# Chunked attention feeding a snake MLP: key blocks at pitch 128, memory keys first, one load per block

## The chip, the cores and the metric

One Trainium2 chip, one core of it. The metric is the time of one execution in microseconds of device time, the median of the runs of a kernel. Its engines are TensorE (PE in the profile, its weight loads PEld), VectorE (DVE), ScalarE (ACT), GpSimd (POOL) and SyncE (SP), which run side by side and wait for each other through semaphores. SP, ACT and POOL also issue DMA transfers. Matrix results land in PSUM, which has 8 banks.

## The reference

```python
# q, k, v: (4, 8, 768, 64); mem_k, mem_v: (4, 8, 8, 64); f32
for c in range(S // 32):                       # chunks of 32 queries
    l_start, r_end = max(0, 32 * c - 16), min(S, 32 * c + 32 + 8)
    k_full = concat(mem_k, k[l_start:r_end])   # 8 memory rows, 16 left, 32 own, 8 right
    v_full = concat(mem_v, v[l_start:r_end])
    a = softmax(q_c @ k_full.T / 8)
    out[32 * c:32 * c + 32] = a @ v_full
x = out.transpose(0, 2, 1, 3).reshape(3072, 512)
h = x @ w_in                                   # w_in: (512, 2048)
g = h + sin(alpha * h) ** 2 / alpha
result = g @ w_out                             # w_out: (2048, 512)
```

## The kernel before

**Attention.** The 768 queries of a batch are taken in 8 blocks `j` of 96 (three chunks). A block needs 8 memory keys and 120 sequence keys, from 16 rows before it to 8 after it, together 128. Scores are computed with keys on partitions and queries on columns: the stationary operand is a slice of 128 columns of `kT` (keys transposed, 64 dims of two heads on 128 partitions), the moving one 96 columns of `qT`. What a chunk may not see is masked by a bias of the exponential (`biasm`, batches 1 to 3, `scores`) or by an extra matmul with `mrow` and `mind` (batch 0, `u_scores`). The value rows of the same 128 keys stand in `vw`, one column of ones beside 64 values, so that `values` (or `u_values`) gives numerators and sums in one matmul; `normed` (DVE, a reciprocal and a multiply) makes `x_blk`, which is transposed into `xT` by TensorE and a copy (words `t`, `T`) or by a DMA transpose from SP (word `c`).

**Layout.** For batches 0 and 1, `kT` holds the sequence with the 8 memory keys repeated every 104 columns, so that neighbouring blocks share columns and a block's slice starts at 104 j; memory keys stand in the middle, at rows 64 to 72 of a block. `vw` and `kst` have the same order: rows 0 to 64, memory, rows 72 to 128. Each is filled by two loads, 64 and 56 rows high.

**How k and q are turned.** Batches 0 and 1: rows lie as `(p r)` with r = 6 on 128 partitions (`k_bf`, `q_bf`); `turn` makes 12 TensorE transposes for a pair of heads `hp` into one PSUM bank, `put_k` (one copy, and a small one for the ends) and `put_q` put them into place. Batch 0's k and q come as f32 by SP (`load_f`, eight loads) and are cast by ACT and DVE (word `a`); batch 1's are cast in the DMA by POOL (`load_one`). Batches 2 and 3: `row_loads` brings rows by POOL into `kst` (16 loads of k) and `qst` (6 of q), `mem_rows` adds the memory keys, and `crosses` turns them by 14 DMA transposes from SP.

**The MLP.** For a batch and one of 16 tiles `ft` of 128 hidden units: `half_tile` (L424) makes 4 matmuls of 384 columns for each half of the batch, `sine` (ACT, L439) takes sin, `squared` squares it on ACT (L444), DVE or POOL (L447), `finish` (DVE, L451) writes `gT` and frees the tile's pair of banks. `second` (L462) makes 96 matmuls of 512 columns per batch, and `close` copies the sum out and stores it.

**The order** is written by hand, as words that `Stage.run` follows; each engine works through its own instructions in that order. Stage -1 is the start and batch 0's attention; stage i is batch i's MLP with batch i+1's attention in it; stage 3 has no attention, and the rest of `second` follows it. Words: `b4`, `h4` the halves of tile 4 (`h` also its sine), `q4A` its square and on which engine (A, V = DVE, P = POOL), `g4` its finish; `f7` seven matmuls of the batch's `second`; `k1 l1` turns of heads 2 and 3, `K1V L1A` their copies; `s24` scores and exponentials of blocks 2 and 4, `v4` values and normalization; `V024` V of batch 0, heads 2 to 4; `I02` w_in tiles 0 and 1; `U12` w_out; `dk108` batch 1's k; `dm` mem_v; `m0` memory values into `vw`; `R2` two of the `row_loads`, `Z` the memory rows, `X8` eight `crosses`; `z1` a dummy matmul on zeros; `Cb` and the like constants.

## Time and profile before

| | |
|---|---|
| time, median of 3 runs | 219.95 us (219.74 to 222.44) |
| span of the profiled execution | 218.5 us; its own time is not listed apart, the median lies 1.45 us above the span |
| TensorE busy | 203.2 us, 93% |
| ScalarE, VectorE, GpSimd busy | 143.6, 140.7, 99.0 us |
| DMA packets | 95908, of them 84864 under 512 bytes |
| POOL's DMA queue | 68736 packets, 13.25 MB |
| the other queue (SP, ACT) | 26976 packets, 14.62 MB |
| first MLP matmul (L424) | 25.14 us from the span's start |
| MLP stages 0, 1, 2, 3 start | 25.1, 75.9, 122.4, 173.3 us |

The page gives the busy time of each engine, then the span in 40 slices of 5.46 us with tenths of busy time (9 is 90% or more) and the granted TensorE clock, then DMA, the chain of waits that ended last, the costliest groups of instructions and the DMA issues. A group's line has its busy time, the mean of one in ns, and after the bar the idle time of the engine just before them and what ended it. Matmuls are pipelined, so the distance of starts, not the mean of one, is what a matmul costs.

### The profile page before, as it was taken

The numbers are of one execution on the slowest core, as the hardware profiler recorded it, in microseconds if no ns is written. First come the engines' busy times: TensorE is split into PE (matmuls) and PEld (weight loads), VectorE is DVE, ScalarE is ACT, GpSimd is POOL, SyncE is SP. The second block draws the span as 40 slices with busy tenths as digits, with TensorE's granted clock in tenths as the row PEclk, the third lists the DMA queues.
The fourth block names the chain that finished last, engine by engine and source line by source line (L and its number), as shares of the span: only waits on it lengthen the run. The fifth ranks groups of instructions, "written<-read, shape, count | busy, mean of one in ns | idle before, by whom it ended". The sixth has DMA issues, their size and how long they took to land.

```text
span 218.5 us, 4460 instructions
## 1 busy us (share of the span) xinstructions
PE 203.2 (93%) x1702; PEld 115.7 (53%) x1721; DVE 140.7 (64%) x218; ACT 143.6 (66%) x230; POOL 99.0 (45%) x140
## 2 busy tenths in 40 slices
PE   0999899999999999999999999994999999999994
PEld 0666655655455555554455555542455465654453
DVE  6697688999353669958577399991165277955010
ACT  2478988977838579969815598865457189892110
POOL 8949506498596490039960087598000004200000
PEclk9999999999999999999999999998899999999999
DMA  6999999999999799939995489999165410000312
GB/s 206 311 167 145 200 209 204 205 153 171 151 179 115 148 143 152 154 74 140 175 188 86 123 75 147 158 89 115 58 154 122 102 51 0 1 3 0 144 48 96
DMA packets 95908, 28.19 MB, mean 129 GB/s; under 512 B 84864, under 2 KB 92432, under 8 KB 95888
## 3 DMA queue, kind: packets, MB, share of 16 engines
q0 software_dynamic: 68736, 13.25, 87.2%
q1 hardware_dynamic: 26976, 14.62, 28.8%
q8 instruction: 13, 0.21, 0.4%
q10 hardware_dynamic: 176, 0.04, 0.1%
q14 instruction: 7, 0.06, 0.1%
HBM read 29.66 MB, written 6.29 MB: 165 GB/s over the span
## 4 chain that ended last, share of the span: by engine, by line
PE 64%; DMA 14%; DVE 7%; POOL 6%; issue 4%; ACT 3%; DVEq 0%; POOLq 0%
PE ps L462 36%; PE ps L424 22%; DMA vw<-in_v_dram 5%; DMA qT<-q_bf 3%; DVE gT L451 3%; DMA q_bf<-in_q_dram 3%; PE ps L414 3%; PE ps L385 2%; DMA kT<-kst 2%; DVE s L447 2%; POOL s L447 2%; ACT u L439 2%; PE ps L366 1%; DMA kst<-in_k_dram 1%; POOL vw L172 1%
## 5 line engine op out<-in xcount | busy, mean ns | idle before, releaser
L462 PE MATMUL ps<-w_out_sb,gT 128*128 128x512 bf16 (+1 forms) x382 | 88.6, 375 | 1.3 <-issue 0.3
L424 PE MATMUL ps<-xT,w_in_sb 128*128 128x384 bf16 x512 | 85.9, 326 | 0.7 <-DVE gT L451 0.5
L451 DVE SCALAR_TENSOR_TENSOR gT<-s,inv_alpha,ps 128x768 bf16<-128x768 f32 x64 | 63.0, 1012 | 12.5 <-ACT s L444 5.2
L424 PEld LDWEIGHTS <-w_in_sb 128*128 128x128 bf16 x512 | 49.7, 98 | 35.2 <-issue 1.8
L439 ACT ACTIVATE u<-ps,alpha_sb 128x768 f32<-128x768 f32 x64 | 56.6, 894 | 16.8 <-PE ps L424 14.3
L462 PEld LDWEIGHTS <-gT 128*128 128x128 bf16 x400 | 37.6, 99 | 38.4 <-issue 2.5
L447 POOL TENSOR_TENSOR s<-u 128x768 f32<-128x768 f32 x11 | 17.4, 1581 | 75.0 <-ACT u L439 75.0
L399 ACT ACTIVATE pt<-ps,biasm 128x256 bf16<-128x256 f32 x72 | 27.3, 488 | 12.1 <-PE ps L385 12.1
L469 DVE COPY o_sb<-ps 128x512 f32<-128x512 f32 (+1 forms) x15 | 9.9, 669 | 32.4 <-PE ps L462 30.5
L447 DVE TENSOR_TENSOR s<-u 128x768 f32<-128x768 f32 x23 | 21.9, 954 | 7.7 <-ACT u L439 7.6
L444 ACT ACTIVATE s<-u 128x768 f32<-128x768 f32 x30 | 25.0, 841 | 0.5
L354 DVE TENSOR_TENSOR x_blk<-ps,rinv 96x512 bf16<-96x512 f32 x32 | 22.0, 686 | 1.1
L469 ACT COPY o_sb<-ps 128x512 f32<-128x512 f32 (+1 forms) x10 | 5.7, 572 | 24.9 <-PE ps L462 24.9
L172 POOL DMA_DIRECT2D vw<-in_v_dram x13 | 12.6, 970 | 8.3 <-PE ps L366 5.3
L353 DVE RECIPROCAL rinv<-ps 96x8 f32<-96x8 f32 x32 | 6.4, 199 | 13.3 <-PE ps L414 12.7
L232 POOL DMA_DIRECT2D kst<-in_k_dram x16 | 11.7, 734 | 1.9 <-DMA vw<-in_v_dram 1.3
L179 POOL DMA_DIRECT2D vw<-in_v_dram x13 | 12.5, 958 | 0.0
L238 POOL DMA_DIRECT2D kst<-in_k_dram x16 | 11.7, 730 | 1.6 <-DMA vw<-in_v_dram 1.4
L369 ACT COPY xT<-ps 128x384 bf16<-128x384 bf16 x12 | 5.6, 495 | 8.0 <-PE ps L366 8.0
L245 POOL DMA_DIRECT2D q_bf<-in_q_dram x12 | 10.7, 909 | 0.0
L414 PEld LDWEIGHTS <-pt 128*128 128x128 bf16 x192 | 8.2, 97 | 4.2 <-ACT pt L399 0.3
L414 PE MATMUL ps<-vw,pt 128*128 128x65 bf16 x192 | 8.9, 193 | 0.0
(81 smaller groups left out, 134.9 us busy)
## 6 DMA issues: line engine op xcount, KB each, us to landing
out_dram<-o_sb SPq DMA_DIRECT2D x23, 256.0 KB, 2.3
kq_f<-in_k_dram SPq DMA_DIRECT2D x4, 384.0 KB, 7.3
kq_f<-in_q_dram SPq DMA_DIRECT2D x4, 384.0 KB, 6.7
q_bf<-in_q_dram POOLq DMA_DIRECT2D x12, 128.0 KB, 6.4
w_in_sb<-in_moe_w_in_dram POOLq DMA_DIRECT2D x1, 1152.0 KB, 12.4
vw<-in_v_dram POOLq DMA_DIRECT2D x7, 128.0 KB, 7.2
vw<-in_v_dram POOLq DMA_DIRECT2D x8, 112.0 KB, 7.5
kst<-in_k_dram POOLq DMA_DIRECT2D x14, 64.0 KB, 4.8
```

Of the source, the lines that this page charges most:

```text
L172: nc.gpsimd.dma_start(vw[0:64, lo:c1, 0:D], win(vflat, a, n, 64))
L179: nc.gpsimd.dma_start(vw[72:128, c0:hi, 0:D], win(vflat, base + QW * c0 + 48, hi - c0, 56))
L354: nc.vector.tensor_tensor(out=x_blk[:].rearrange("p g e d -> p e g d"), in0=otv[0:QW, :, :, 0:D], in1=rinv[:].unsqueeze(3).to_broadcast([Q ...
L399: nc.scalar.activation(pt[:, 0:H * QW].rearrange("p (g e c) -> p g e c", g=2, e=4)[:, :, :, 32 * m:32 * m + 32], sc[:, :, 0:4 * QW].rearra ...
L414: nc.tensor.matmul(otv[:, e, hp, :], pt[:, QW * i:QW * i + P], vws[b % 2][:, 2 * hp + e, j, 0:D + 1],)
L424: nc.tensor.matmul(t["hT"][:, hf, 0:HALF], w_in_sb[:, kt, P * t["ft"]:P * t["ft"] + P], t["xT"][:, kt, HALF * hf:HALF * hf + HALF], start= ...
L439: nc.scalar.activation(t["u"][:], t["hT"][:, :, 0:HALF], ACTF.Sin, scale=alpha_sb[:, ft:ft + 1])
L444: nc.scalar.activation(s2[:], u[:], ACTF.Square)
L447: e.tensor_tensor(out=s2[:], in0=u[:], in1=u[:], op=ALU.mult)
L451: nc.vector.scalar_tensor_tensor(out=gT[:, ft, :].rearrange("p (e c) -> p e c", e=2), in0=t["s2"][:], scalar=inv_alpha[:, ft:ft + 1], in1= ...
L462: nc.tensor.matmul(o[:, c0:c1], gT[:, ft, P * s:P * s + P], w_out_sb[:, ft, c0:c1], start=(ft == 0), stop=(ft == FT - 1),)
L469: copier(state["engines"][state["o"] % len(state["engines"])])(o_sb[:, c0:c1], o[:, c0:c1])
```

## The change

Blocks of `kT` stand at pitch 128 for all batches, with the 8 memory keys (and values, and `kst` rows) first, then the 120 sequence rows. So a block of V or of key rows is one load of 120 rows in place of two: 16 loads of k for batches 2 and 3 instead of 32, one V load per word instead of two. k and q of batches 0 and 1 lie with r = 8 on 96 partitions, k in the memory of `kst`; `turn` makes 16 transposes of 96 columns, for k with zero columns before and after, and `put_k` makes one copy of 120 columns a block (in halves of four blocks for batch 0). Of batch 0 only heads 0 and 1 come by SP as f32; the other six pieces are cast by DMA in POOL's queue, in one order with V, and six casts on ACT and DVE go. Constants move from POOL to DVE, and the masks are built by memsets. All five orders are new. Squares by engine (A, V, P) before: 6, 7, 3 in stage 0, 9, 6, 1 in stage 1, 6, 6, 4 in stage 2, 9, 4, 3 in stage 3; after: 8, 5, 3; 8, 7, 1; 9, 4, 3; 11, 3, 2. Copies of kT in stage 0: two on ACT and two on DVE before, three and one after. Dummy matmuls in the start: 11 before, 26 after. Matmuls of `second` ahead of batch 3's first scores (`s24`): 14 before, 30 after.

```diff
+    pts_all = consts.tile([P, NPT, H * QW + 32], BF, name="pts")
+    pts = [pts_all[:, i, :] for i in range(NPT)]
     memv_st = consts.tile([P, B, H, D], BF, name="memv_st")
     kst = consts.tile([P, NJ, H * D], BF, name="kst")
-    k_bf = consts.tile([P, H, 6, D], BF, name="k_bf")
-    q_bf = consts.tile([P, H, 6, D], BF, name="q_bf")
-    qst = q_bf[:].rearrange("p h r d -> p (h r d)").rearrange("p (t c) -> p t c", t=NSUB)
+    k_bf = kst[:].rearrange("p a (b d) -> p a b d", d=D)
+    q_bf = consts.tile([P, H, 8, D], BF, name="q_bf")
...
+            dst[0:QW, h0:h1].rearrange("p h r d -> p h (r d)"),
+            src[b, h0:h1].rearrange("h (p r) d -> p h (r d)", p=QW),
...
-        vf = v[b].rearrange("h (j t) d -> t (h j) d", t=QW)
         vflat = v.rearrange("b h s d -> (b h s) d")
-        base = b * H * S
         c0, c1 = h0 * NJ, h1 * NJ
-        lo = c0
-        if c0 == 0 and b == 0:
-            nc.gpsimd.dma_start(vw[16:64, 0:1, 0:D], vf[0:48, 0:1])
-            lo = 1
-        a = base + QW * lo - 16
-        n = c1 - lo
-        nc.gpsimd.dma_start(
-            vw[0:64, lo:c1, 0:D], win(vflat, a, n, 64)
-        )
-        hi = c1
+        row = b * H * S + QW * c0 - LEAD
+        if row < 0:
+            nc.gpsimd.dma_start(vw[NM + LEAD:P, 0:1, 0:D], win(vflat, 0, 1, P - NM - LEAD))
+            c0, row = 1, QW - LEAD
         if c1 == H * NJ and b == B - 1:
-            nc.gpsimd.dma_start(vw[72:120, c1 - 1:c1, 0:D], vf[48:96, c1 - 1:c1])
-            hi = c1 - 1
-        nc.gpsimd.dma_start(
-            vw[72:128, c0:hi, 0:D], win(vflat, base + QW * c0 + 48, hi - c0, 56)
-        )
+            c1 -= 1
+            nc.gpsimd.dma_start(
+                vw[NM:NM + LEAD + QW, c1:c1 + 1, 0:D],
+                win(vflat, b * H * S + QW * c1 - LEAD, 1, LEAD + QW),
+            )
+        nc.gpsimd.dma_start(vw[NM:P, c0:c1, 0:D], win(vflat, row, c1 - c0, P - NM))
...
+            lo = max(0, QW * j - LEAD)
+            hi = min(S, QW * j - LEAD + P - NM)
+            r0 = NM + lo - (QW * j - LEAD)
+
+            def one(j=j, lo=lo, hi=hi, r0=r0):
                 nc.gpsimd.dma_start(
-                    kst[r0:64, j, :].rearrange("p (h d) -> p h d", d=D),
-                    k[b, :, lo + r0:lo + 64, :].rearrange("h p d -> p h d"),
+                    kst[r0:r0 + hi - lo, j, :].rearrange("p (h d) -> p h d", d=D),
+                    k[b, :, lo:hi, :].rearrange("h p d -> p h d"),
                 )
-
-            def two(j=j, n=n):
-                nc.gpsimd.dma_start(
-                    kst[72:72 + n, j, :].rearrange("p (h d) -> p h d", d=D),
-                    k[b, :, QW * j + 48:QW * j + 48 + n, :].rearrange("h p d -> p h d"),
-                )
-            todo += [one, two]
+            todo.append(one)
...
+    def turn(src, hp, n, r, lead=0, tail=0):
         bank, bs = banks.single()
-        t = bank[:, 0:384].bitcast(BF).rearrange("p (r c) -> p r c", r=6)
-        for r in range(6):
+        w = (lead + n + tail) // r
+        t = bank[:, 0:r * w // 2].bitcast(BF).rearrange("p (r a) -> p r a", r=r)
+        pads = bank[:, 0:r * w // 2].rearrange("p (r a) -> p r a", r=r)
+        for lo, hi in ((0, lead), (lead + n, lead + n + tail)):
+            if hi > lo:
+                c0, c1 = lo // (2 * r), hi // (2 * r)
+                nc.tensor.matmul(
+                    pads[:, :, c0:c1], zeros[:, 0:P],
+                    zeros[:, 0:r * (c1 - c0)].rearrange("p (r a) -> p r a", r=r)
+                )
+        for i in range(r):
             for e in range(2):
                 nc.tensor.transpose(
-                    t[64 * e:64 * e + 64, r, :], src[:, 2 * hp + e, r, :], ident[:]
+                    t[64 * e:64 * e + 64, i, lead // r:(lead + n) // r],
+                    src[0:n // r, 2 * hp + e, i, :], ident[0:n // r, 0:n // r]
                 )
         return t, bs
 
-    def copier(eng):
-        return nc.scalar.copy if eng == "A" else nc.vector.tensor_copy
-
-    def put_k(b, hp, tb, eng="A"):
+    def turn_k(hp):
+        return turn(k_bf, hp, S, 8, LEAD, LEAD)
+
+    def turn_q(hp):
+        return turn(q_bf, hp, S, 8)
+
+    def put_k(b, hp, tb, eng, j0, j1):
         t, bs = tb
-        kT = kTs[b % 2]
+        r, w = t.shape[1], t.shape[2]
         copier(eng)(
-            kT[:, hp, 72:72 + 7 * 104].rearrange("p (s c) -> p s c", c=104)[:, :, 0:96]
-            .rearrange("p s (a r) -> p s a r", r=6),
-            t[:, :, 8:120].rearrange("p r (s a) -> p s a r", a=16),
-        )
-        ends = kT[:, hp, 16:912].rearrange("p (s c) -> p s c", c=112)[:, 0:8:7, 0:48]
-        nc.vector.tensor_copy(
-            ends.rearrange("p s (a r) -> p s a r", r=6),
-            t.rearrange("p r (s a) -> p s a r", a=8)[:, 0:16:15],
-        )
-        banks.give(bs)
-
-    def put_q(b, hp, tb, eng="V"):
+            kTs[b % 2][:, hp, P * j0:P * j1].rearrange("p (s c) -> p s c", c=P)[:, :, NM:P]
+            .rearrange("p s (a r) -> p s a r", r=r),
+            bass.AP(tensor=t.tensor, offset=t.offset + QW // r * j0,
+                    ap=[t.ap[0], [QW // r, j1 - j0], [1, (P - NM) // r], [w, r]]),
+        )
+        if j1 == NJ:
+            banks.give(bs)
+
+    def put_q(b, hp, tb, eng, c0, c1):
         t, bs = tb
+        r = t.shape[1]
         copier(eng)(
-            qTs[b % 2][:, hp, :].rearrange("p (a r) -> p a r", r=6),
-            t.rearrange("p r a -> p a r"),
-        )
-        banks.give(bs)
-
-
+            qTs[b % 2][:, hp, c0:c1].rearrange("p (a r) -> p a r", r=r),
+            t[:, :, c0 // r:c1 // r].rearrange("p r a -> p a r"),
+        )
+        if c1 == S:
...
-    for hp in (1, 2, 3):
-        load_f(k, hp, kq_f[hp])
-        load_f(q, hp, kq_f[4 + hp])
...
-        'a1A Cb Cp Cz Cv a5A eVA Cm Cl z4 a0V Ci k0 dm a4V l0 k1 K0V Ck l1 L0A V024 We L1V a2A K1A V002 '
-        'a6V k2 s00 K2V a3V s11 V068 m0 a7V s01 l2 s10 k3 K3A L2A V046 z4 v10 l3 Cs L3A I02 v11 z1 s20 '
-        'v01 s30 v00 z1 s31 v30 s21 z1 v31 T01 T10 v20 T30 T00 v21 T20 T31 I27 t11 t21 eVA Ws '
+        'Cv z1 aq0A z1 Cp z1 z1 dm z1 Cz z1 ak0V Cb z3 k0 m00 z1 K00A dk024 K01A dq024 k1 z1 V002 l0 '
+        'dq046 K10V L00V dk068 z1 Ci Cm Ck dk046 z1 V024 l1 K11V L01V z1 s00 m01 z1 z1 v00 L1A s01 z3 '
+        's10 s11 k2 l2 V046 K20V L2A dq068 z1 K21V v10 V068 k3 I27 v11 s21 T00 I02 s20 v01 l3 K30A '
+        'K31V L3A v21 z1 v20 z1 t10 s30 s31 T11 Cl v30 z1 v31 z3 Ws T20 T21 t31 t30 t01 '
     ))
...
-        'o8 b0 h0 I7g q0V U69 U12 b1 h1 dq108 q1A b4 h4 b3 g0 h3 b6 g1 dk108 q4V g4 q3A b2 h2 h6 b5 h5 '
-        'Ufg g3 b7 q2V U01 U56 q6P h7 g2 q5A b10 U24 q7P g6 h10 b9 q10A g5 h9 U45 b8 h8 g7 g10 q8A q9V '
-        'V158 b11 h11 g9 b13 g8 h13 l0 l2 l3 L0A L2A q13P k2 q11V Ube b15 U9b g11 Uef g13 K2V h15 b12 '
-        'q15V h12 q12A b14 g15 f7 h14 V125 k1 k0 g12 l1 K1V k3 L1V L3A q14V K3A K0A V102 f9 g14 s61 f16 '
-        'm1 s70 s3 f13 v0 f3 v6 c6 f6 v3 f5 s542 T3 f10 T0 v4 f6 v2 f2 v1 c4 c2 f7 v7 f1 T1 f3 v5 Ws T7 '
-        'f8 t5 '
+        'b0 I7g h0 b1 o8 h1 b3 b4 q0V U12 q1A h4 g0 g1 q4V h3 g4 U69 b6 b2 q3A dq108 g3 U01 h2 q2V h6 '
+        'b5 dk108 Ufg h5 b7 U24 U9b U56 q5A q6P h7 g2 b10 q7P h10 g6 q10A b8 g5 b9 h9 g7 g10 h8 V158 '
+        'q9V U45 b11 q8A h11 Ube g9 b13 h13 g8 l0 l2 L2A L0V l3 q13A q11V k2 g13 K2A g11 b15 h15 q15A '
+        'V102 b12 h12 b14 g15 h14 l1 q12A g12 f7 k1 f2 L3A k0 m1 Uef k3 V125 L1A K1V f6 K0A K3A q14P '
+        'f3 g14 s61 f16 s3 s70 f11 v6 c6 f1 v0 f3 v3 f2 f5 s542 Cs f10 v4 t3 f3 Ws v1 t0 v2 c2 f2 c4 '
+        'f13 t1 f1 v7 f1 f4 v5 f6 f6 t5 t7 f5 '
...
-        'b3 Ws R9 b0 h0 R1 h3 b5 h5 Ws R1 b1 q5A q0V g0 R2 q3P g3 h1 Ws q1A b2 h2 g5 R1 g1 b4 h4 R1 b6 '
-        'q4A q2V h6 g2 R1 Z b7 h7 b9 h9 R1 g4 R1 q6V b8 g6 R1 eV o1 h8 q7P g7 q8A b11 h11 X1 q11A q9P b10 '
-        'g9 g8 h10 b13 g11 h13 R1 q10V g10 b14 h14 b12 q13P X3 V305 h12 g13 q12V q14A R1 f8 eAV b15 g12 '
-        'R1 H3 h15 f6 g14 q15V X8 s24 f16 g15 f2 s103 f9 v4 v0 f3 X1 f2 X1 c4 v3 f2 c3 v2 f1 c2 f6 c0 '
-        's675 f10 v1 f4 c1 Ws f1 v7 v5 c7 v6 f2 c6 c5 f24 '
+        'R1 b3 Ws R9 b0 h0 h3 b5 h5 b1 q0V q3P q5A Ws h1 g0 b2 Ws g3 q1A R2 h2 g5 b4 g1 h4 R1 R1 R1 b6 '
+        'q4A h6 q2V g2 eV R1 b7 Z R1 h7 g4 q6V b9 R1 h9 b8 h8 g6 o1 q7P q9P q8A g7 b11 g8 h11 b10 X1 '
+        'g9 q11A h10 b13 R1 q10A h13 g11 b14 q13A V305 b12 g10 X3 h14 g13 h12 q14V q12A H3 b15 h15 f1 '
+        'R1 f7 q15A g14 X1 R1 f16 R1 g12 f6 g15 X8 s24 f1 f7 s103 f2 f2 v4 f2 eAV c4 f1 v0 f1 f1 f2 f1 '
+        'v3 X1 f5 v2 f1 c3 f1 c2 f4 c0 f6 s675 f3 v1 f4 v7 c1 f5 Ws v6 c7 c6 v5 c5 f24 '
-        'b2 h2 q2V b0 h0 b4 q0A g2 h4 b3 h3 g0 o2 b1 h1 Ws q3P b6 q4V q1A h6 g4 b8 h8 g3 b5 g1 q6A h5 q5A '
-        'b7 g6 h7 b11 q8P g8 h11 b10 g5 q7V h10 q10A q11P b9 h9 q9A g7 g11 b12 h12 b15 g10 q12A h15 g9 '
-        'g12 b13 h13 b14 q15A h14 g15 q14A q13V g14 g13 '
+        'b0 b2 h2 q2V h0 b4 q0A h4 g2 b3 h3 o2 q4A q3P b1 g0 Ws h1 b6 q1A h6 g4 b8 h8 g3 g1 b5 q6A h5 '
+        'q8P b7 g6 q5A h7 g8 b11 h11 g5 b10 q11A h10 b9 q10A q7V h9 q9A g7 b12 g11 h12 g10 b15 q12A '
+        'h15 b13 q15A g9 h13 g12 b14 h14 q14A q13V g14 g13 g15 '
```

159 lines of the change are left out of this document (66 added, 93 removed), and 10 rows, old and new, of the table stage.

## The prediction

> **What bounds the kernel now.** I read the page first (engine totals, the slices), then who TensorE waited for, the chain of waits in order of time, the engines by stretch, the timelines of 0 to 64 us and 120 to 200 us, and the DMA issues with their time to landing.
>
> ```profile
> PE 203.2 (93%) x1702; PEld 115.7 (53%) x1721; DVE 140.7 (64%) x218; ACT 143.6 (66%) x230; POOL 99.0 (45%) x140
> ...
> PE   0999899999999999999999999994999999999994
> ...
> PEclk9999999999999999999999999998899999999999
> DMA  6999999999999799939995489999165410000312
> ```
>
> TensorE is the bound from the first MLP tile to the end, with one hole, slice 28 of 40. Before that tile DMA is the busy resource. The chain of waits shows what an unhindered matmul costs and the hole:
>
> ```profile
> 143.48 6.63 DMA qT<-q_bf
> 150.11 0.14 issue
> 150.25 0.35 PE ps L385 x8
> 150.59 4.60 PE ps L462 x13
> ...
> 185.38 9.26 PE ps L424 x56
> 194.64 0.21 PE ps L462
> 194.85 0.05 issue
> 194.91 10.74 PE ps L462 x49
> ```
>
> A 384-column L424 takes 9.26/56 = 0.165 us, a 512-column L462 10.74/49 = 0.219 us. After the hole 13 of the latter took 4.60 us, not 2.85. TensorE's list of waits names it:
>
> ```profile
> PE ps L753 <- DVE mcol L746: 4.6, 1, 4.6
> PE ps L385 <- DMA qT<-q_bf: 3.1, 1, 3.1
> ```
>
> And POOL's own:
>
> ```profile
> POOL vw L172 <- DMA memv_st<-in_mem_v_dram: 3.0, 1, 3.0
> ```
>
> The first wait lies in the start, where DMA is the limit anyway. The second is batch 3's scores waiting for turned q rows. The third is POOL's ninth load, held until its first had landed: eight loads are in flight at most. By stretch (start, stages 0 to 3, end; us from the span's start):
>
> ```profile
> 0.00:25.10 25.10, 18.13 (x288) 12.55 (x289) 19.88 (x54) 15.85 (x24) 20.40 (x50) 1.00 1.70 206
> 25.10:75.90 50.80, 49.90 (x469) 28.76 (x473) 35.53 (x52) 38.30 (x64) 30.42 (x38) 1.00 1.62 174
> 122.40:173.30 50.90, 47.29 (x350) 25.39 (x352) 29.91 (x42) 34.12 (x57) 21.36 (x23) 0.97 1.12 110
> 173.30:194.60 21.30, 21.08 (x130) 12.61 (x129) 16.21 (x17) 18.17 (x23) 4.43 (x3) 1.00 0.07 26
> ```
>
> Columns: PE, PEld, DVE, ACT, POOL busy, clock, DMA share, GB/s. TensorE is full in stages 0 and 3 (0.9 and 0.2 us idle), and ACT comes next: in stage 3 it is busy for 18.2 of 21.3 us. Most prices below are from these rows:
>
> ```profile
> L451 DVE SCALAR_TENSOR_TENSOR gT<-s,inv_alpha,ps 128x768 bf16<-128x768 f32 x64 | 63.0, 1012 | 12.5 <-ACT s L444 5.2
> L439 ACT ACTIVATE u<-ps,alpha_sb 128x768 f32<-128x768 f32 x64 | 56.6, 894 | 16.8 <-PE ps L424 14.3
> L447 POOL TENSOR_TENSOR s<-u 128x768 f32<-128x768 f32 x11 | 17.4, 1581 | 75.0 <-ACT u L439 75.0
> L447 DVE TENSOR_TENSOR s<-u 128x768 f32<-128x768 f32 x23 | 21.9, 954 | 7.7 <-ACT u L439 7.6
> L444 ACT ACTIVATE s<-u 128x768 f32<-128x768 f32 x30 | 25.0, 841 | 0.5
> ```
>
> **The change, part by part.**
>
> *Start, the loads.* Before, SP brings eight f32 pieces of k and q (3.1 MB written) and V follows: the last V load lands at 15.99 + 6.1 = 22.1 us, the first w_in piece 0.9 later, at 23.0, and the first L424 starts at 25.14. After, two pieces stay on SP; six are cast by DMA in POOL's queue, each half the bytes. Landings in that queue come one after the other, so I add gaps between landings. SP's two: from 2.4, 1.5 each (3.9 and 5.4 us in before) = 3.0. mem_v: 0.25 (estimate: 256 packets at V's rate). Six casts: batch 1's 768 KB took 3.6 (k_bf) and 4.6 (q_bf), so 0.90 to 1.15 per 192 KB; w_out's 384 KB in packets of the same 1 KB took 1.96, 0.98 per 192 KB, which I take: 5.9. V: 5744 packets in 5.56 us between two landings, so 7680 take 7.45; single loads of 120 rows have the same packets as pairs of 64 and 56. w_in: now columns 2 to 7 first (3.64), then 0 to 2 (0.92). Sum 2.4 + 3.0 + 0.25 + 5.9 + 7.45 + 3.64 + 0.92 = 23.6 (23.1 to 24.6 by the ends). POOL's issues keep ahead: ident to 1.3, 13 loads at 0.55 to 1.1 and the mind operations (1.8) put the last V issue at 14.3, five us before its data end; the memsets of L726, L797, L792, L801 (1.6 us on POOL) go to DVE. The limit of eight in flight holds the ninth until mem_v is down, now by 5 us, so it no longer bites.
>
> *Start, the engines.* DVE: the masks (ten small memsets and three copies, some 1.3 us instead of the 2.9 of L733 to L746) and six casts gone; kT in halves of 480 elements at 0.65 (between L285's 672 in 0.854 and L291's 96 in 0.254). First exponentials at about 11.9 (mind from POOL at 9.0, the mem-key columns at 10.7, 0.8 for L332). Then 12.4 + eight normalizations at 0.91 (L353 and L354 pitch) + three halves + four xT copies at 0.35 + 0.45 for alpha = 23.4. Both ledgers agree: the first L424 at 23.5 instead of 25.14, **-1.65**. The extra dummy matmuls (26 for 11) stand ahead of nothing that is ready sooner.
>
> *Stage 0.* Each turn of k or q is 16 transposes of 96 columns for 12 of 128 (36 took 1.10 us, 0.37 a turn): 0.37 by columns, 0.49 by count, at most 8 x 0.12 = 1.0 us more and two tiny pad matmuls; I take 0.43. ACT gets two squares more (6 to 8) and three whole kT copies of 960 elements (0.96 by L285 and L299 on ACT) for two of 672 (0.72): 16 x 0.894 + 8 x 0.841 + 3 x 0.80 + 3 x 0.96 = 26.3 us where it was 23.1. Before, ACT needed 26.64 to 52.83 for its 23.1, so 3.1 was waiting. Walking after's order through, sine by sine and bank pair by bank pair, I find 1.4 of waiting left: the last kT copy ends 1.4 + 26.3 + 1.4 = 29.1 after the first L424, and batch 1's scores, which TensorE would reach at 128 x 0.1655 + 8 x 0.43 + 16 x 0.219 = 28.1, start at 23.5 + 29.3 = 52.8 to 53.0 for 53.73. Of 1.65 us **0.8** is left.
>
> *Stage 1.* The eight key loads that go (L238) free 8 x 0.73 us of POOL and nothing waits on that: batch 2's 14 transposes are paced by SP at 1.3 us each, ended in time before and start with the stage. POOL's memsets of kst (1.1 us) now stand behind a square and batch 1's last turn, ahead of those loads; the loads still land over 10 us before the first transpose. 0 (bounds -0.5 and +0.5).
>
> *Stage 2.* Before, POOL issued 22 loads around four squares, and the sixth q load left at 145.87; the transposes (eight kT from 127.06, then q) ended too late for s24 at 146.82. After there are 14: eight keys and two q right after batch 3's V pieces (about 97 to 105 us), the other four q directly behind the first square (about 125 to 129), and V305 only after two more squares (its 4800 packets, some 5 us, and the eight copies of H3 behind it, 5.1, end before s24). So SP's row is the limit: the mem-key rows leave as early as before less 0.8 (122.5), kT from 126.2, q from 136.8 at 1.3 each; the fourth q tile is down by 146 even at the 6 us that the slow ones took. s24 stands behind 30 second-layer matmuls instead of 14, so TensorE is there at about 121.6 + 21.2 + 30 x 0.219 = 149.4. The wait goes, 3.1, and the slow matmuls after it, 1.75. What is late next: only 66 instead of 82 of these matmuls are left to cover the softmax of eight blocks; walking the banks I find waits of 0.2, 0.1 and 0.35. ACT's three extra squares (2.5 us) lie beside those 30 matmuls. **-4.85 + 0.65 = -4.2** (bounds -4.85 and -1.4, where all 16 moved matmuls, 3.5 us, come back as a wait).
>
> The 1.75 rests on the row: a clock of 0.66 in 150 to 155 us after a gap of 3.08. [...]
>
> *Stage 3.* No loads; ACT has 11 squares for 9. Sine and square pitch 0.91 and 0.75: walking the order, the last square ends 24.95 us after the stage's start (23.8 before) and the last gT 27.9. TensorE is held by banks for about 0.6, then reaches the matmul that needs that gT at 28.0. **+0.6** (bounds 0 and +1.7, both squares at full price).
>
> *Sum.* 218.5 - 0.8 - 4.2 + 0.6 = 214.1 us of span. The profiled execution's own time is not listed; the median of 219.95 lies 1.45 above the span, so **215.5 us**.
>
> **The rivals.**
> *The start comes through whole:* casts at 0.90, the first L424 at 23.1, ACT's waiting in stages 0 and 3 smaller than walked. For it: ACT waited 3.1 us there. Against: its work rises by 3.2. -2.0 - 4.85 + 0: 211.65 + 1.45 = 213.1.
> *The start gives nothing* because it is DMA-bound as before: casts at 1.15, w_in's first columns behind 640 others, L424 at about 25. For it: w_in's first piece was needed at 23.0 and is planned for 23.6. Then ACT makes stage 0 later by 0.6: 218.5 + 0.6 - 4.2 + 0.6 = 215.5, and 217.0 with 1.45. That is also the case in which the change does not do what the moved loads promise.
> *The hole moves:* s24 no longer waits, but stage 3's first tiles do, for batch 3's last xT, since 16 matmuls went ahead. For it: the last xT transpose landed at 173.7, just at stage 3's start. Against: the first half tile needs blocks 0 to 3 only. 215.5 + 3.5 = 219.0.
> *Slower: ScalarE becomes the bound.* It gains 3.2 us in stage 0, 3 x 0.841 = 2.5 in stage 2, 2 x 0.841 = 1.7 in stage 3, 7.4 in all. If all of it is on the path, 218.5 - 1.65 - 4.85 + 7.4 = 219.4, 220.9 us. It decides from 6.5 of the 7.4. Against: DVE and POOL give up as much, and 30 matmuls cover stage 2.
>
> **How the numbers follow.** Forecast 0.45, whole start 0.18, no start 0.18, moved hole 0.12, ScalarE 0.07. 2% (about what a measurement of this kernel can tell from no change) is 215.55: half of the forecast's chance, the whole start and a little of the third give 0.44 faster; beyond 224.35 lies only the tail of the last two, 0.05; the rest, 0.51, is within. The range takes in the whole start with the lower ends of stage 1 (-0.5) and of the turns (-0.5), and the moved hole: 212.0 to 219.6.
>
> **What would show it.** Right: the first L424 near 23.5; L385 missing from the DMA waits and no slice of lower PEclk after the start; batch 1's first scores waiting for an ACT kT copy; stage 3 about 0.6 longer with ACT nearly full. Wrong: a wait of L424 for w_in_sb before 25 us, TensorE waiting for xT at stage 3's start, gaps over 0.3 us before L424 released by DVE gT.

## The result, and the profile after

The changed kernel is slower: 231.34 us (median of 4 runs, 229.94 to 233.48) beside 221.19 us for the kernel before in the same comparison; the ratio is 1.044, with a 95% interval of 1.035 to 1.053. The ratio leaves out the run of 233.48 us, which is more than 1.5% above the fastest run of its kernel. The prediction said 215.5 us, with a range of 212.0 to 219.6. The profiled run took 230.45 us, with a span of 228.7. The line numbers have moved: the MLP's first matmul is now L414 (it was L424), its second L452 (L462), the scores L375 (L385), the values L404 (L414), gT L441 (L451), the dummy matmuls L674 (L686), the copy of the mem-key rows into kst L229 (L253), the key and query turns by DMA L236 and L239 (L260 and L263).

The page first, its engine totals and the rows of the slices that answer to those of before:

```profile
PE 212.4 (93%) x1796; PEld 118.4 (52%) x1816; DVE 135.6 (59%) x214; ACT 144.8 (63%) x228; POOL 82.4 (36%) x97
...
PE   6699799999988999999499999999999999999994
...
PEclk9769999999999999999679999999999999999999
DMA  7999999999999999459998333999634430000312
```

POOL is relieved (82.4 us for 99.0) and the hole of slice 28 has gone. But there is a new one in slice 20 of 40, with a low clock in that slice and the next, and the start has slices of 6 and 7. The low clock in the start is not new, although the row of the kernel before shows 9 there: a dummy matmul of 512 columns took 0.63 us at 5.9 to 7.8 us in the kernel before and 0.38 from 15.8 us on, against 0.60 at 9 to 15 us and 0.38 from 22 us on in the changed kernel. TensorE's list of waits has the new hole first and waits of the start behind it:

```profile
PE ps L375 <- DMA qT<-q_bf: 3.7, 1, 3.7
PE ps L262 <- DMA kst<-in_k_dram: 1.2, 1, 1.2
PE ps L674 <- DVE zeros L708: 1.2, 1, 1.2
PE ps L262 <- DVE biasm L721: 1.1, 1, 1.1
```

The first is the same wait as before, scores for a turned query tile, but now batch 2's in stage 1 and no longer batch 3's in stage 2. Stages are measured here from one stage's first MLP matmul to the next one's (for the kernel before 25.14, 75.70, 122.28 and 173.30 us):

| stretch | before | after | difference | predicted |
|---|---|---|---|---|
| start | 25.14 | 28.48 | +3.3 | -1.65 |
| stage 0 | 50.56 | 53.01 | +2.45 | +0.85 |
| stage 1 | 46.58 | 53.74 | +7.15 | 0 |
| stage 2 | 51.02 | 47.24 | -3.8 | -4.2 |
| stage 3 and end | 45.2 | 46.2 | +1.0 | +0.6 |
| span | 218.5 | 228.7 | +10.2 | -4.4 |

The chain of waits of the changed kernel tells where stage 1's 7 us come from (start, duration, what):

```profile
82.59 6.73 DMA kst<-memv_st
89.39 1.55 SPq L236
...
100.18 1.22 SPq L239
101.48 1.22 SPq L239
102.79 1.63 SPq L239
104.52 7.24 DMA qT<-q_bf
112.40 3.10 PE ps L452 x7
115.94 3.43 PE ps L452 x12
```

The mem-key rows of batch 2 were issued 1.1 us after the stage's start, as in before, but took 6.73 us to land, where the trace of before has 4.5 (76.76 to the first kT turn at 81.3). Three V loads of 120 rows had been issued between 79.89 and 82.61 and were still in flight until 84 to 92 us. SP's fourteen turns, 1.3 us each, so started 7.9 us into the stage, where before they started 5.7 us into it, and the query turns ran into the next transfers: V268 and V357, issued at 103.02 and 104.24, and batch 3's key loads from 105.41. The fourth query tile, issued at 104.52, took 7.24 us, where an undisturbed turn takes 2.4. TensorE was at the scores at 107.9 and waited until 111.8. By stretch (columns as in the prediction: length, then PE, PEld, DVE, ACT, POOL busy, clock, DMA share, GB/s):

```profile
81.50:107.90 26.40, 26.15 (x155) 14.64 (x154) 20.60 (x23) 21.56 (x30) 8.57 (x8) 1.00 1.12 111
107.90:112.00 4.10, 0.44 (x13) 0.32 (x14) 3.17 (x4) 1.84 (x5) 4.10 (x5) 0.83 2.14 134
112.00:120.00 8.00, 8.00 (x59) 3.23 (x59) 1.29 (x2) 2.71 (x7) 3.16 (x4) 0.66 2.62 143
```

Up to the wait the stage is as long as before (26.4 us, 26.35 in before). Then come the wait and 8 us at a mean clock of 0.66, in which 19 matmuls of the second layer took 6.53 us; at the 0.219 us each of the full clock they would take 4.2.

In the start the first exponentials begin at 14.31 us (13.11 in before; the prediction had 11.9). ScalarE's timeline, with the idle time before an instruction in brackets:

```profile
7.21 1.04 ACT L640 CAST q_bf<-kq_t 96x1024 bf16<-96x1024 f32 x1 [3.87 <-DMA kq_t<-in_q_dram]
8.16 1.00 ACT L277 COPY kT<-ps 128x480 bf16<-128x480 bf16 x2
14.31 0.81 ACT L321 ACTIVATE pts<-ps 128x768 bf16<-128x768 f32 x1 [5.15 <-DVE vw L182]
```

and TensorE's of the same time:

```profile
8.31 0.85 PE L262 MATMUL ps<-ident,kst 96*64 96x96 bf16 x16 [1.24 <-DMA kst<-in_k_dram]
9.09 0.61 PE L674 MATMUL ps<-zeros 128*128 128x512 bf16 x1
9.63 0.85 PE L262 MATMUL ps<-ident,q_bf 96*64 96x96 bf16 x16
```

The first query turn stands behind the second key turn, whose rows come by a cast in the DMA queue and land only at 8.27. The query rows themselves were ready for TensorE at 8.25. The first exponentials name a copy on VectorE as what released them; the scores that they read (L314) ended at 14.28, at about the same time.

### The profile page after: what moved, and what is told of

The parts are those of the page before. It is cut to its first block, busy times and chain, and to the rows that moved or that the text cites. A ratio compares the mean times of both kernels' runs of the same rounds, so it can differ in the third digit from the quotient of the medians.

```text
span 228.7 us, 4583 instructions
## 1 busy us (share of the span) xinstructions
PE 212.4 (93%) x1796; PEld 118.4 (52%) x1816; DVE 135.6 (59%) x214; ACT 144.8 (63%) x228; POOL 82.4 (36%) x97
## 4 chain that ended last, share of the span: by engine, by line
PE 56%; DMA 10%; ACT 9%; DVE 9%; issue 6%; SPq 6%; POOL 1%; DVEq 0%; POOLq 0%; ACTq 0%
PE ps L452 32%; PE ps L414 13%; SPq L236 4%; ACT u L429 4%; DVE gT L441 4%; DMA qT<-q_bf 3%; DMA kst<-memv_st 3%; PE ps L404 3%; DMA kst<-in_k_dram 3%; PE ps L262 2%; PE ps L375 2%; SPq L239 2%; ACT pts L389 2%; DVE s L437 2%; ACT s L434 2%
## 5 line engine op out<-in xcount | busy, mean ns | idle before, releaser
L452 PE MATMUL ps<-w_out_sb,gT 128*128 128x512 bf16 (+1 forms) x383 | 90.2, 377 | 2.0 <-issue 0.8
L414 PE MATMUL ps<-xT,w_in_sb 128*128 128x384 bf16 x512 | 86.5, 326 | 1.1 <-DVE gT L441 0.6
L441 DVE SCALAR_TENSOR_TENSOR gT<-s,inv_alpha,ps 128x768 bf16<-128x768 f32 x64 | 62.7, 1011 | 15.5 <-ACT s L434 10.5
L414 PEld LDWEIGHTS <-w_in_sb 128*128 128x128 bf16 x512 | 49.7, 98 | 36.3 <-issue 3.7
L452 PEld LDWEIGHTS <-gT 128*128 128x128 bf16 x400 | 37.1, 99 | 38.4 <-issue 3.6
L389 ACT ACTIVATE pts<-ps,biasm 128x256 bf16<-128x256 f32 x72 | 27.5, 486 | 20.0 <-PE ps L375 20.0
L434 ACT ACTIVATE s<-u 128x768 f32<-128x768 f32 x36 | 30.3, 842 | 0.9
L437 DVE TENSOR_TENSOR s<-u 128x768 f32<-128x768 f32 x19 | 18.4, 970 | 9.9 <-ACT u L429 9.8
L459 ACT COPY o_sb<-ps 128x512 f32<-128x512 f32 (+1 forms) x9 | 5.1, 565 | 23.5 <-PE ps L452 23.4
L175 POOL DMA_DIRECT2D vw<-in_v_dram x13 | 17.6, 1354 | 0.8 <-PE ps L404 0.8
L214 POOL DMA_DIRECT2D kst<-in_k_dram x16 | 15.2, 976 | 0.8 <-DMA vw<-in_v_dram 0.8
L404 PEld LDWEIGHTS <-pts 128*128 128x128 bf16 x192 | 8.3, 97 | 6.0 <-ACT pts L389 2.3
L321 ACT ACTIVATE pts<-ps 128x768 bf16<-128x768 f32 x8 | 6.4, 812 | 7.4 <-DVE vw L182 5.2
L674 PE MATMUL ps<-zeros 128*128 128x512 bf16 x23 | 9.6, 519 | 1.4 <-DVE zeros L708 1.2
L375 PE MATMUL ps<-qT,kT 64*128 64x96 bf16 x192 | 6.8, 209 | 3.7 <-DMA qT<-q_bf 3.7
L404 PE MATMUL ps<-vw,pts 128*128 128x65 bf16 x192 | 9.6, 193 | 0.6 <-ACT pts L389 0.6
```

Of the source, the lines that this page charges most:

```text
L175: nc.gpsimd.dma_start(vw[NM:P, c0:c1, 0:D], win(vflat, row, c1 - c0, P - NM))
L214: nc.gpsimd.dma_start(kst[r0:r0 + hi - lo, j, :].rearrange("p (h d) -> p h d", d=D), k[b, :, lo:hi, :].rearrange("h p d -> p h d"),)
L389: nc.scalar.activation(pt[:, 0:H * QW].rearrange("p (g e c) -> p g e c", g=2, e=4)[:, :, :, 32 * m:32 * m + 32], sc[:, :, 0:4 * QW].rearra ...
L404: nc.tensor.matmul(otv[:, e, hp, :], pt[:, QW * i:QW * i + P], vws[b % 2][:, 2 * hp + e, j, 0:D + 1],)
L414: nc.tensor.matmul(t["hT"][:, hf, 0:HALF], w_in_sb[:, kt, P * t["ft"]:P * t["ft"] + P], t["xT"][:, kt, HALF * hf:HALF * hf + HALF], start= ...
L434: nc.scalar.activation(s2[:], u[:], ACTF.Square)
```

## The experiments

All start from the changed kernel unless said otherwise. Each theory was put down before the run. From e1 to e8, and in e11 and e12, a kernel was run once, so their spans are those of one execution.

### First study: four causes, one at a time

**e1_vorder**: batch 2's V loads earlier in stage 1.

```
-  ... h9 dy Z q9A ... eV V378 V226 g11 ... b14 V202 h14 ...
+  ... h9 dy V226 V202 Z q9A ... eV V378 g11 ... b14 h14 ...
```

> Batch 2's V loads of blocks 2 to 6 (words V226 and V202) are issued some 10 us earlier in stage 1, right behind batch 1's V rows for the mem rows and ahead of word Z, instead of just ahead of batch 2's mem-key rows. Theory A: in the changed kernel batch 2's mem-key rows (L229) landed 6.7 us after their issue (4.5 in the kernel before) because these V loads of 3840 packets were in flight; the key turns, and behind them the query turns, then ran until batch 2's V and batch 3's key loads were in flight as well, and TensorE waited 3.7 us for a query tile at 107.9. So here the mem-key rows land in 3.5 to 4.7 us, no wait of L375 for qT over 1 us is left, no slow clock follows, stage 1 (first L414 to first L414) takes 47 to 48 us instead of 53.7, the span is about 222.5. Rival A2: the query turns are stretched by batch 2's later V loads and batch 3's loads themselves, wherever the mem-key rows stand: a wait of 2 us or more and a slice of low clock stay, stage 1 takes 51 to 54 us, span 227 to 229.

Span 227.7, as the rival had it; stage 1 took 49.23 us, between the two. The wait of the scores was gone, but a new one stood at the head of stage 1, where it counts in stage 0's stretch (55.36 us for 53.01):

```profile
PE ps L414 <- DMA xT<-x_blk: 2.2, 1, 2.2
```

POOL had nothing to do at that time, so the V loads left at 71.81 and 73.52, not behind V378, and were in flight when SP turned batch 1's last xT blocks: the one that TensorE waited for was issued at 77.05 and landed 7.67 us later. The mem-key rows still landed in 5.1 us, and the kT turns started only 0.75 us sooner. So this run did not do what it was meant to do. It moved the same stretch from one turn to another, and the scores no longer waited mostly because V268 left later: at 107.96 for 103.02, while the fourth query turn left at 103.02 for 104.52. It does show that V loads in flight stretch SP's turns, and that neither order had room for them.

**e2_split**: the pairs of loads (64 and 56 rows) put back.

```
-  dma_start(vw[NM:P, c0:c1, 0:D], win(vflat, row, c1 - c0, P - NM))
+  dma_start(vw[NM:72, c0:c1, 0:D], win(vflat, row, c1 - c0, 64))
+  dma_start(vw[72:P, c0:c1, 0:D], win(vflat, row + 64, c1 - c0, 56))
   # and the key rows in the same way
```

> Each V block load and each key row load is issued as two again (64 and 56 rows), at the new pitch and in the new orders; everything else as in the changed kernel. Theory: single loads or pairs carry the same packets, so the start's first L414 stays within 0.7 us of 28.5 and stage 1 within 1.5 us of 53.7; span 228 to 231 (POOL's issues cost it 0.5 us per pair more). Rival: a single 120-row load holds the DMA engines against the turns, and splitting takes away most of stage 1's wait of 3.7 us: stage 1 at 47 to 50 us, span 222 to 225.

Span 227.3; the first L414 at 28.71, stage 1 52.40. The theory held for the start and the stage, with the span a little under what it said: splitting changes the start by 0.2 and stage 1 by -1.3, and two waits of the scores (1.1 and 2.1) remain.

**e3_f32**: all of batch 0's k and q as f32 pieces through SP again.

```
-  ... K00A dk024 K01A dq024 k1 z1 V002 l0 dq046 ...
+  ... K00A ak1A K01A aq1V k1 z1 V002 l0 ...      # ak2V aq2A ak3V aq3A further on
```

> All eight f32 pieces of batch 0's k and q come by SP again and are cast by ScalarE and VectorE, the other words of the start stand as in the changed kernel. Theory B: the casts by DMA slow the start (the first k and q pieces land at 5.18 and 7.18 instead of 3.86 and 5.38, the DMA moves 160 to 190 GB/s in the first 8 us instead of 206 to 298): the first pieces land within 0.4 us of the old times, the first exponentials come by 13.2, the first L414 at 25.3 to 26.3 instead of 28.48, span about 226. Rival B2: the start's time is set by TensorE's order and by the dummy matmuls at half clock, not by the loads: the first L414 stays at 27.5 to 29, span 228 to 229.5.

Neither: the first L414 came at 42.13, the span was 243.1. With the six casts out of POOL's queue its V loads left earlier, the first large one at 3.04 us, and shared the DMA with SP's f32 pieces. The chain begins with it:

```profile
3.04 16.38 DMA vw<-in_v_dram
```

It took 16.4 us, and the f32 pieces came in up to 16.5 (14.9 in before, where POOL's first V load left at 5.74). The first values waited for it until 19.47 us (they began at 15.18 in the changed kernel). Behind them TensorE waited another 6.7 us for the casts on ScalarE and VectorE, which stand in an order that was not made for them, at a mean clock of 0.50 from 12 to 28 us. So the run does not decide on the casts by DMA as a whole. It does show that without them in POOL's queue SP's first two pieces landed at 4.95 and 6.81, hardly sooner than at 5.18 and 7.18.

**e4_nodummy**: the start's dummy matmuls after the first nine left out.

> The dummy matmuls of the start behind the first nine are left out; everything else as in the changed kernel. Theory C: the dummies ran at half clock, 0.6 us each, in TensorE's order between 9 and 16 us, ahead of the turns and scores; without them the first exponentials come at 13 to 13.6 instead of 14.31 and the first L414 at 26.5 to 27.7 instead of 28.48. Rival C2: they stand where TensorE waits for loads or for VectorE anyway, and keep its clock up: the first L414 stays at 28.2 or comes later (up to 30), with a granted clock under 0.9 in more of the first 28 us.

The first L414 at 28.38 for 28.48, span 228.4, so the rival held, in its second half too: from 16 to 20 us the granted clock was 0.50, where the changed kernel has 1.00. The dummies stand where TensorE waits anyway, and the slower clock without them made the start no longer.

### Second study: the hole and the order of the start

**e5_memrows**: only the mem_k rows (dy) and their copy into kst (Z, here Y) move, from stage 1 to stage 0.

```
-  ... s542 Cs f10 v4 ...          (stage 0)      ... h9 dy Z q9A ...  (stage 1)
+  ... s542 Cs dy Y f10 v4 ...                    ... h9 q9A ...
```

> The mem_k rows of batches 2 and 3 (word dy) and the copy of batch 2's mem-key rows into kst (word Z) move from stage 1 to stage 0, right behind the memsets of kst; V and key loads stay where they are. The first study moved V loads instead, and the stretch went to batch 1's xT turns, so it left open whether the late mem-key rows alone make the hole. Theory A: the mem-key rows land at about 70 to 76 us, the first kT turn issues as soon as SP's earlier stores have gone (82 to 83 us, 6 to 7 earlier than 89.39), all query turns land ahead of V268's and batch 3's key traffic, L375 waits for no query tile, no slow clock follows; stage 1 takes 46.6 to 47.5 us, the span is 221.5 to 222.5. Rival A2: the V loads in flight between 80 and 92 us stretch the turns whenever they start: a wait of 2 us or more stays and stage 1 takes over 50 us.

Theory A held. SP's first kT turn left at 84.16, 0.9 us after the stage's start (7.9 in the changed kernel). With the V loads in flight that turn took 8.8 us, but kT turns have time; the query turns were issued from 97.88, the fourth at 101.81, ahead of V268 at 104.79. The scores of stage 1 wait for nothing and the clock stays full:

```profile
83.26:109.70 26.44, 26.19 (x155) 14.68 (x156) 20.63 (x23) 21.61 (x30) 8.63 (x8) 1.00 1.60 125
109.70:115.00 5.30, 5.30 (x50) 2.38 (x51) 4.34 (x6) 3.95 (x11) 5.30 (x6) 1.00 2.85 140
```

Stage 1 took 47.57 us for 53.74. So 6.2 of the 10.2 us go with this one order in this execution. The only wait for a query tile that is left is in stage 2, which is 0.55 us longer:

```profile
PE ps L375 <- DMA qT<-q_bf: 0.5, 1, 0.5
```

The span fell only to 224.7, because the start, which has the same words, ended at 30.23 here. Over the four kernels with the unchanged start (the changed one, e1, e5, e7) the first L414 lies between 28.46 and 30.23, so differences under 2 us in the start need more than one kernel.

**e6_start**: the order of the start alone.

```
-  z3 k0 m00 z1 K00A dk024 K01A dq024 k1 z1 V002 l0 dq046 K10V L00V dk068 z1 Ci Cm Ck dk046 ...
+  z3 k0 Cm Ck K00A dk024 K01A dq024 l0 z1 L00V V002 Ci k1 dk046 dq046 s00 L01V K10V s01 V024 l1 ...
```

> Only the order of the start changes: query turn 0, the mask row and the mem-key columns stand ahead of key turn 1 in TensorE's order, the scores ahead of the values, batch 0's key and query casts by DMA in order of head pairs, w_in's first two columns of tiles ahead of the rest. The loads are the same. Theory D: the start of the changed kernel was set by TensorE's order (scores behind turns whose casts by DMA had not landed, later scores behind values), the loads only behind that. Then the first exponentials come at 10.5 to 12 instead of 14.31, the last V load lands at 21.5 to 22, the first L414 starts at 25 to 26 instead of 28.48, span 225 to 226.5. Rival D2: the DMA sets it: the first exponentials come earlier but VectorE and TensorE then wait for V, and the first L414 stays at 27.5 or later.

Part of each. The first exponentials came at 11.66, as theory D said:

```profile
8.51 1.01 ACT L277 COPY kT<-ps 128x480 bf16<-128x480 bf16 x2
11.66 1.51 ACT L321 ACTIVATE pts<-ps 128x768 bf16<-128x768 f32 x2 [2.15 <-PE ps L314]
```

The last V load landed at 21.20, yet the first L414 came at 27.39, not at 26 or before; the span was 222.7. This start stands in three more kernels below, in two of them with one or two edits more, with the first L414 at 26.54, 26.23 and 26.81. That is 1.7 to 2.2 us better than the least of the four above, and this run 1.1. The rest, some 1.4 us over before, lies in the order as well or in the later landing of the first pieces; I have not told them apart.

The run gives something else by chance. It leaves the mem-key rows where the change put them, but its stage 1 took 49.09 us for 53.74, with a wait of only 1.5 us and no slow clock behind it:

```profile
106.00:109.00 3.00, 1.45 (x20) 0.71 (x20) 2.90 (x5) 2.58 (x6) 3.00 (x5) 1.00 2.58 112
109.00:112.00 3.00, 3.00 (x21) 1.32 (x22) 1.80 (x3) 2.29 (x6) 2.88 (x3) 1.00 2.20 144
112.00:116.00 4.00, 3.95 (x40) 1.97 (x39) 1.66 (x4) 2.23 (x7) 2.14 (x3) 1.00 2.64 149
```

So an edit that does not touch stage 1 took 4.65 us off it. Here the fourth query turn left 0.35 us behind V268 (102.22 and 101.88), in the changed kernel 1.5 us behind it: the size of the hole hangs on about a microsecond.

**e7_stage0**: work from ScalarE to VectorE in stage 0.

```
-  l1 q12A g12 f7 k1 f2 L3A k0 m1 Uef k3 V125 L1A K1V f6 K0A K3A q14P f3 g14 s61 f16
+  l1 q12V g12 f7 k1 f2 L3A k0 Uef k3 V125 L1A K1V f6 K0V K3A q14P f3 g14 s61 m1 f16
```

> In stage 0 one square (q12) and one kT copy (K0) go from ScalarE to VectorE, and batch 1's mem-value copy stands behind them. Theory: batch 1's first scores wait for ScalarE's last kT copy, as the prediction had it, so they start 0.4 to 1.0 us earlier than 29.84 after the first L414, stage 0 takes 52.0 to 52.6 instead of 53.0. Rival: TensorE's own order sets it (the turns behind second-layer matmuls), no change, 52.9 to 53.1.

The rival held: the first scores of batch 1 came 29.80 us into the stage for 29.84, and the stage is as long as in the changed kernel (52.98 us for 53.01). ScalarE now idles where it was busy, and what it waits for is TensorE:

```profile
53.34 1.49 ACT L289 COPY qT<-ps 128x768 bf16<-128x768 bf16 x2
56.78 0.96 ACT L277 COPY kT<-ps 128x960 bf16<-128x960 bf16 x1 [1.95 <-PE ps L262]
57.75 1.28 ACT L389 ACT_TABLE_LOAD   x1
```

**e8_all**: these three edits together.

> The three edits of the other runs together. If each is worth what its theory says and they don't touch: the first L414 at 25 to 26, stage 0 at 52 to 52.6, stage 1 at 46.6 to 47.5, stages 2 and 3 as in the changed kernel, span 217.5 to 219.5, about level with the kernel before. If the gains of the start are taken back by stage 0 (its w_out and batch 1 loads come no earlier), span 220 to 222.

Span 220.3, its run 222.04 us, with the kernel before at 220.87 beside it. The hole is gone (stage 1 47.56), the first L414 at 26.54, stage 0 52.93, stages 2 and 3 as in the changed kernel. By stretch the gains of the parts about add up, but the mended kernel still doesn't beat the one before.

### Third study: the gain of stage 2, and the last pieces

**e9_before_r**: the kernel before, with nine loads of stage 2 moved together.

```
-  ... R2 q3P g3 h1 Ws q1A b2 h2 g5 R1 g1 b4 h4 R1 b6 ... R1 Z ... R1 g4 R1 q6V b8 g6 R1 ... R1 ... R1 ... R1 H3
+  ... R2 q3P R9 g3 h1 Ws q1A b2 h2 g5 g1 b4 h4 b6 ... Z ... g4 q6V b8 g6 ... H3
```

> The kernel before with one edit: in stage 2 the last nine of batch 3's key and query loads stand together right behind POOL's first square instead of one by one behind later squares and V305. Layout, pairs of loads and every other order as in the kernel before. Theory S: the hole of the kernel before was POOL's order alone (the fourth query tile's load left at 137.35 and landed at 143.46, its turn then fell behind V305's traffic), not the pairs of loads. Then L385 waits for no query tile at s24, no slow clock follows, stage 2 takes 46.3 to 47.2 us instead of 51.0, stages 0, 1 and 3 stay, the span is 213.7 to 214.7, the ratio to before 0.975 to 0.985: faster than both kernels. Rival S2: 22 loads are too many to land in time whatever the order, the query turns stay late: stage 2 over 49 us, span over 216.5.

Theory S held in the profile: stage 2 took 46.89 us for 51.02, all other stretches are within 0.15 us of before, and the span is 214.5. The list of waits has no L385 for a query tile, and the page no hole and no slow clock:

```profile
PE   0899899999999999999999999999999999999994
...
PEclk9999999999999999999999999999999999999999
```

The fourth query load left at 132.53 for 137.35 and its turn at 143.07, just ahead of V305. In 12 runs this kernel took 215.43 to 217.09 us, median 216.37, with the span between 213.7 and 215.3. The 19 runs of the kernel before that were timed beside it lie in two groups: sixteen of 219.73 to 222.24 us, at a mean granted clock of 0.984 to 0.992, and three of 215.73, 216.49 and 217.83, at 1.00. The ratio counts only those three, and against them it is 1.001 (0.998 to 1.005), so the expected 0.975 to 0.985 is not confirmed as a verdict. Over all runs the medians stand at 216.37 to 220.35. Both profiles of the kernel before (the second is e12) are of the longer group and show the gap and the clock; there is no profile of a short run. Their clock tells something: in the profile the clock is 0.50 for 3.4 us behind the gap and 1.00 around it, which makes a mean of 0.992 over the span, an estimate from these two numbers. So the sixteen runs at 0.984 to 0.992 look like runs with one or two such stretches and the three at 1.00 like runs without, and with the edit all twelve are at 0.998 or more. The edit so seems to make sure of what the kernel before reaches in three runs of 19.

**e10_best**: e8 with the mask operations ahead of POOL's first load, and the last stage in the words of the kernel before.

```
-  z1 Cp z1 z1 dm ... V002 Ci k1 ...      b0 b2 h2 q2V h0 b4 q0A h4 g2 b3 h3 o2 q4A q3P ...
+  z1 Cp Ci z1 z1 dm ... V002 k1 ...      b2 h2 q2V b0 h0 b4 q0A g2 h4 b3 h3 g0 o2 ...
```

> The changed kernel with the mended start, mem-key rows and stage 0 of the fourth run of the last study, and two edits more, read by stage. First: the mask operations (word Ci) stand ahead of POOL's first load. If POOL's loads in flight are what made the first f32 pieces land at 5.2 and 7.2 to 7.6 us instead of 3.86 and 5.38, then they land by 4.3 and 6.0, the first exponentials come at 10 to 11 instead of 11.69 and the first L414 at 25 to 26.2 instead of 26.54; if the f32 pieces' own form (96 partitions of 2 KB rows) does it, they land as late as now and the first L414 is no earlier. Second: the last stage has the words of the kernel before. The prediction gave its new order +0.6 us; then stage 3 and the end go from 46.1 back to 45.2 to 45.5. Span 218 to 219.3, ratio to before about 1.00.

Its four runs took 222.44 to 227.01 us; the ratio to the kernel before is 1.038 (1.019 to 1.057), against those same three short runs. The profiled run is the shortest of the four, with a span of 220.7, over the expected 219.3; another run at a mean clock of 1.00 took 225.59, so the spans of single runs in this document can lie some 3 us off. POOL's first load left at 3.01 us for 1.55, and q0 still landed at 7.22, which speaks against POOL's loads as what delays the first pieces. The first L414 came at 26.23. The second edit was a miss of another kind: stage 3 and the end took 46.8 us, 0.7 more than with the new words, because of a wait that the new words avoid:

```profile
PE ps L414 <- DMA xT<-x_blk: 1.1, 1, 1.1
```

The old order opens stage 3 with both halves of tile 2, and the new stage 2 ends its xT turns later. Without this wait the old words would take 45.7, an estimate, so the new order's own price is about 0.4.

### Fourth study: two small questions

**e11_halfrows**: as e10 in the start, stage 3 as in e8, and each f32 piece in two loads.

```
+  for c0 in (0, 4 * D):
+      nc.sync.dma_start(t[0:QW, :, c0:c0 + 4 * D], src[:, :, c0:c0 + 4 * D])
```

> The mended kernel (fourth run of the second study) with the mask operations ahead of POOL's first load and each of SP's two f32 pieces brought in two loads of 1 KB rows instead of one of 2 KB rows. In the last study POOL's first load at 3.0 us changed nothing: k0 landed at 5.1, q0 at 7.2. If the 2 KB rows are what is slow, k0 is down by 4.5 and q0 by 6.2 us; if it is the 96 partitions (or anything else that both forms share), they land as late as before, 5.0 to 5.6 and 7.0 to 7.8. First L414 at 25.5 to 26.6, stages as in the mended kernel.

Neither, with k0 down at 4.77 and q0 at 6.53, half of the way. The first L414 came at 26.81, the span was 220.8. The cause is not settled.

**e12_before**: the kernel before, once more.

> The kernel before, unchanged, for a second profile: of its 19 timed runs three took 215.7 to 217.8 us at a mean granted clock of 1.00 and sixteen 219.7 to 222.2 at 0.984 to 0.992. If the clock's answer to the gap is what differs, stage 2 shows the same wait of L385 of 2.5 to 3.3 us in both, and a slice of low clock only in the longer runs; if the gap itself comes and goes with the timing of the loads, a short run shows no wait of L385 above 1 us. A long run again would show stages within 0.5 us of the first profile and leave it open.

A long run again (220.31 us, clock 0.992): the same wait, 2.9 us. Stage 0 took 51.43 us for 50.56, more than the 0.5 us that was expected at most, the other stages are within it.

```profile
PE ps L385 <- DMA qT<-q_bf: 2.9, 1, 2.9
```

Why three of 19 runs are 2.5 to 4.6 us shorter than the median stays open.

## Why the prediction was wrong, step by step

*Stage 1, "0 (bounds -0.5 and +0.5)"*: the step that failed most, by 7.15 us. It looked at how early the key loads land ("over 10 us before the first transpose") and took the turns to "start with the stage". They start once the mem-key rows are down, which are a DMA of their own on SP, and the new order puts that DMA behind V loads that were not in flight in the same amount before. 2.2 us of lateness there were enough, because V268, batch 3's keys and the query turns were already side by side: in the kernel before the fourth query turn left 0.46 us ahead of V268, in the changed kernel 1.5 us behind it. e5 moves the mem-key rows alone and gets 6.2 of the 7.15 back. The other traces bear out that this distance decides. Wherever the fourth query turn of stage 1 left ahead of V268 (both profiles of the kernel before, e1, e5, e8 to e11), the scores did not wait; where it left behind, by 0.35 (e6), 1.08 (e4), 1.40 (e7), 1.50 (changed kernel), 1.82 (e3) and 1.96 us (e2), they waited for 1.5, 3.4, 3.7, 3.7, 5.3 and 3.2 us in all. The hole of the kernel before in stage 2 is the same: there the turn left 1.03 us behind V305, in e9 0.07 us ahead of it. In stage 2 of the changed kernel the turn left 4.4 us behind V305 and the scores still did not wait, with 30 matmuls ahead of them for 14, as the prediction had it. The prediction had a rival with a moved hole, but looked for it in stage 3. In the changed kernel stage 3 has no such wait; e10 shows that it does appear there, with 1.1 us, once the last stage's old words are put back.

*Start, the loads, "23.6"*: w_in's first columns landed at 25.46. The two f32 pieces were taken at 1.5 us each from before's rows and were down at 7.18 instead of 5.4; pieces of 96 rows of 2 KB are not pieces of 128 rows of 1.5 KB (e10 speaks against POOL's loads as the cause, e11 puts some of it on the row's length). mem_v, casts and V were taken at 13.6 us and took 14.5 (7.18 to 21.66), a small miss. So half the bytes written for six casts saved little at the end: the last V load landed at 21.66 for 22.10, and the columns of w_in that are needed first at 25.46 for 23.02.

*Start, the engines, "Both ledgers agree"*: they were two sums of busy time, and neither engine was busy throughout. VectorE idled 1.33 and 1.72 us at a time behind the values and the key turns, and TensorE's order put scores behind turns and values that were not ready. The sum of 23.4 became 28.5, 3.0 us behind w_in's columns. The order accounts for 1.1 to 2.2 us (e6, e8, e10, e11); the rest is not told apart. That dummies "stand ahead of nothing that is ready sooner" was right (e4).

*Stage 0, 0.85 us given back*: it was 2.45. Up to batch 1's scores the time was close (29.84 us into the stage for 29.3), the reason was not. It was to be ScalarE's last kT copy. e7 takes a square and a copy from ScalarE and gains 0.04. TensorE itself is full: from the first L414 to these scores it spends, by the distance of starts, 4.43 us on turns and their pad matmuls, which was taken at 3.44 and was 3.49 in the kernel before, and 22.0 on L414, taken at 21.2 and 21.5 before. Another 1.2 us go between these scores and stage 1, in waits of up to 0.5 that the prediction did not walk, such as this one of the changed kernel:

```profile
PE ps L452 <- ACT pts L389: 0.5, 1, 0.5
```

*Stage 2, -4.2*: right, -3.8. The scores come 28.15 us into the stage (predicted 27.8) and wait for nothing; the trace has 29 records of the 30 second-layer matmuls ahead of them. What the prediction did not ask is which part of the change does it. e9 has none of the new layout, none of the single loads, and its profile gets 4.1 from the place of nine load words.

*Stage 3, +0.6*: +1.0 with the end; e10 puts about 0.4 of it on the order, the rest is not located.

*The clock*: the prediction took the price of the slow matmuls, 1.75 us, from the row, a gap of 3.08 us and a clock of 0.66 behind it. The runs agree with the row and go further, as the last section shows: behind a wait of 2.2 us (e1) the clock was 0.50 for 3.4 us as well.

*ScalarE as the bound*, the rival on the slower side, did not come out either: ScalarE was busy for 144.8 us of the span for 143.6, and relieving it in stage 0 (e7) gained nothing.

*From span to time, 1.45 us*: in every run on record that lists both it is 1.73 to 1.84, so this term was 0.3 short.

In all: the mended kernel's 220.3 stands against 214.5 for the kernel before without its hole. The difference of 5.8 us is what the change costs apart from its own hole: 1.3 in the start, 2.25 in stage 0, 1.0 in stage 1, 0.3 in stage 2 and 0.9 behind it. These are two single profiles; by all their runs e9 (median 216.37 us) and e10, which is close to the mended kernel (median 225.31), lie further apart.

## What to carry to other kernels

When transfers are reordered, follow the small copy that a chain of transfers starts with, and ask what is in flight at its issue: a delay of 2 us at its head came out as 7 at its end, since the last links met the next batch's loads. A ledger of busy time is a lower bound for an engine that works in order; walk the order with the landing times before believing that two ledgers agree. And before crediting a rewrite with a gain, try the cheapest part of it alone: here nine words in another place did as much in that stage's profile as the whole change.
